# The last two row blocks of a fused attention and feed-forward kernel: product 7 of both blocks ahead of product 4 of both, and the very last rows stored whole

## The chip, the cores and the metric

The kernel runs on one core of one Trainium2 chip. The metric is the device time of one execution in microseconds (us), as a median of several executions. Beside the timed ratio I use a second measure, taken from the profile: the time **from the start of the first matmul of product 7 of row block 0 to the end of the span**. I call it *the end*. Everything that the change touches lies inside it, or at most touches its first moment.

Names in the profile lines: PE is TensorE (matmuls), DVE is VectorE (adds and copies), and SP, ACT and POOL (GpSimd) issue the stores here; a "pair" is the two store issues, of 64 rows each, for one block of 128 rows. A store has landed when the last of its 16 completion signals has arrived.

## The reference, cut to what matters

```python
def reference(q, k, v, omega, w_gate, w_val, w_out):
    attn = performer_attention(q, k, v, omega)        # 8 batches, 8 heads, 576 x 64
    x = attn.transpose(0, 2, 1, 3).reshape(4608, 512)
    g = x @ w_gate                                    # 512 -> 1536
    val = x @ w_val
    return (gelu(g) * val) @ w_out                    # 1536 -> 512, float32
```

Only the last product, for the last rows, matters here.

Of the kernel before, what the change touches and what calls it, by code (L numbers as in the profile page):

```python
# [15 lines left out]
def kernel(  # L16
# [11 lines left out]
    nc = tc.nc  # L28
# [308 lines left out]
    HF, HT = N_DFF // 2, T_TOK // 2  # L337
# [1112 lines left out]
    def end(p):  # L1450

        p.g.sum(0, nc.vector, 0, 3)
        p.g.sum(0, nc.vector, 3, HF)
        p.g.sum(1, nc.vector, 0, HF)
        p.pm(0, 1, 0, HF - 1)
        p.pm(1, 1, 0, HF - 1)
        p.pm(0, 2, 0, HF - 1)
        p.pm(1, 2, 0, HF - 1)
        p.pm(0, 1, HF - 1, HF)
        p.ps_(0, 1, act)  # L1460
        p.pm(1, 1, HF - 1, HF)
        p.ps_(1, 1, act)
        p.pm(0, 2, HF - 1, HF)
        p.pm(1, 2, HF - 1, HF)
        p.g.sum(3, nc.vector, 0, HF)
        p.pm(0, 5, 0, 3)
        p.pm(1, 5, 0, 3)
        p.pm(0, 5, 3, HF)
        p.ps_(0, 5, act)
        p.pm(1, 5, 3, HF)  # L1470
        p.ps_(1, 5, act)
        p.pa(0, 0)
        p.pa(1, 0)
        p.g.sum(2, nc.vector, 0, HF)
        p.pm(0, 6, 0, HF)
        p.ps_(0, 6, act)
        p.pm(1, 6, 0, HF)
        p.ps_(1, 6, act)
        p.pm(0, 3, 0, HF)
        p.pa(0, 1)  # L1480
        p.pst(0, 0, None, (nc.sync, nc.scalar))
        p.pm(1, 3, 0, HF)
        p.pa(1, 1)
        p.pst(1, 0, None, (nc.sync, nc.scalar))
        p.pm(0, 7, 0, HF)
        p.pa(0, 2)
        p.pm(0, 4, 0, HF)
        p.pc(0, dve)
        p.pst(0, 1, None, (nc.sync, nc.scalar))
        p.pm(1, 7, 0, HF)  # L1490
        p.pa(1, 2)
        p.pst(1, 1, 1, (nc.sync, nc.scalar))
        p.pm(1, 4, 0, HF)
        p.pc(1, dve)
        p.pst(1, 1, 0, (nc.sync, nc.scalar))
    E = mybir.EngineType
    with tc.manual_schedule(engines={E.Activation, E.PE, E.DVE, E.SP, E.Pool}):
        g, a = first()
        for t in range(2, N_TOK):
            p = Projection(t - 1, g)  # L1500
            if t + 1 < B:
                n = Attention(t + 2) if t + 2 < B else None
                g, a = step(t, p, a, n), n
            else:
                g = bare(t, p)
        end(Projection(N_TOK - 1, g))
# [30 lines left out]
```

## The kernel before: the parts that the change touches

The kernel takes the 4608 rows in nine groups of 512. The product with `w_out` of the last group is done by a Strassen-like scheme: seven products, numbered 1 to 7, in place of eight, for each of two row blocks `s` (0 and 1) of 128 rows of each half. Product `n` of block `s` is `pm(s, n, ...)`, six matmuls of 128x128 by 128x256. One PSUM tile, `one[s]`, gathers products 1, 6, 7 and 4 one on top of the other, and what it holds is read in between:

```python
def pm(self, s, n, i0, i1):
    ...
    ps = self.two[s][:, 0] if n in (3, 5) else self.two[s][:, 1] if n == 2 else self.one[s]
    for i in range(i0, i1):
        nc.tensor.matmul(ps, x[:, i, s * P:(s + 1) * P], y[:, i], start=n in (1, 2, 5) and i == 0,
                         stop=i == HF - 1, skip_group_check=n not in (1, 2, 5))

def pa(self, s, k):                    # VectorE: o_sb += a PSUM tile
    dst = (self.lo[s][:, :m], self.lo[s][:, m:], self.hi[s][:, m:])[k]
    nc.vector.tensor_add(dst, (self.two[s][:, 1], self.two[s][:, 0], self.one[s])[k], dst)

def pc(self, s, copy):                 # copy one[s], now complete, to the other columns
    copy(self.hi[s][:, :d_model // 2], self.one[s])

def pst(self, s, r, part=None, queues=(nc.sync, nc.sync)):   # store whole rows, or one half of the columns
    ...

def store(c0, o_sb, ns=slice(0, d_model), queues=(nc.sync, nc.sync)):
    for i in range(2):                 # 64 rows each: a pair of issues
        ...
        queues[i].dma_start(out=..., in_=o_sb[i * SP:(i + 1) * SP, :])
```

So `pa(s, 2)` must read `one[s]` after product 7 and before product 4 of the same block. The last lines of the program before the change (cut):

```python
p.pm(0, 7, 0, HF)                               # product 7 of block 0
p.pa(0, 2)                                      # add: reads one[0]
p.pm(0, 4, 0, HF)                               # product 4 of block 0: on top of one[0]
p.pc(0, dve)                                    # copy
p.pst(0, 1, None, (nc.sync, nc.scalar))         # store whole rows
p.pm(1, 7, 0, HF)
p.pa(1, 2)
p.pst(1, 1, 1, (nc.sync, nc.scalar))            # store one half of the columns early
p.pm(1, 4, 0, HF)
p.pc(1, dve)
p.pst(1, 1, 0, (nc.sync, nc.scalar))            # and the other half last
```

The softmax here doesn't subtract the row's maximum and nothing guards it: scores larger than these inputs give would overflow.

## Time and profile before

Times in us after the start of product 7 of block 0, which is at 333.06 of the span (from the trace of before):

| what | block 0 | block 1 |
|---|---|---|
| product 7 starts | 0.00 | 1.99 |
| product 4 starts | 1.33 | 3.32 |
| last copy starts | 2.19 | 4.17 |
| last stores issued (SP and ACT) | 2.64 | 3.29 and 4.62 |
| last landing (SP / ACT) | 4.96 / 5.30 | 6.55 / 6.83 |
| end of the span | | 7.91 |

The median was 343.06 us of three runs, 342.66 to 343.08. The table is read downward: matmuls and VectorE take turns until 4.6, and from there to 7.9 there is only the last store and what follows its landing. The profile lines behind it stand in the prediction.

### The profile page before, as it was taken

How to read it: one execution, taken by the hardware profiler on the slowest of the kernel's cores; microseconds unless marked ns; L12 is line 12 of the kernel's file. 1: busy time of each engine (PE TensorE's matmuls, PEld its weight loads, DVE VectorE, ACT ScalarE, POOL GpSimd, SP SyncE). 2: the span in 40 equal slices, each digit the busy share in tenths (PEclk: the TensorE clock that was granted, in tenths of full speed). 3: DMA queues.
4: the chain of work that ended last, by engine and by line, in shares of the span. 5: the costliest groups of instructions: out<-in, count | busy, mean ns of one | idle time of the engine just before them, and what ended most of it. 6: DMA issues, size and time to landing. Idle time of an engine off the chain costs nothing.

```text
span 341.0 us, 7993 instructions
## 1 busy us (share of the span) xinstructions
PE 327.4 (96%) x3114; PEld 206.0 (60%) x3155; DVE 229.1 (67%) x481; ACT 214.3 (63%) x434; POOL 149.9 (44%) x152
## 2 busy tenths in 40 slices
PE   7889999889999999999999999999999999999994
PEld 3565455566646664566447654665466786686683
DVE  3875388979773768375936683677457777796783
ACT  4894366774778558756875677658765447626640
POOL 8326004033486447744674559477968400000000
PEclk9999999999999999999999999999999999999999
DMA  8999999599889256945498629671413040013004
GB/s 155 275 206 207 206 272 206 137 174 236 178 135 331 49 102 91 326 89 108 60 326 113 116 32 291 164 111 19 94 33 63 8 115 11 1 32 93 2 0 124
DMA packets 67173, 45.08 MB, mean 132 GB/s; under 512 B 47296, under 2 KB 60096, under 8 KB 67136
## 3 DMA queue, kind: packets, MB, share of 16 engines
q0 software_dynamic: 14848, 22.12, 31.4%
q1 hardware_dynamic: 51744, 21.64, 30.4%
q10 hardware_dynamic: 544, 0.82, 0.8%
q8 instruction: 24, 0.39, 0.5%
q14 instruction: 13, 0.11, 0.1%
HBM read 37.78 MB, written 9.44 MB: 138 GB/s over the span
## 4 chain that ended last, share of the span: by engine, by line
PE 83%; DVE 6%; DMA 3%; ACT 3%; issue 2%; POOL 2%; DVEq 0%; POOLq 0%
PE g_ps L433 20%; PE o_ps L559 18%; PE val_one L378 11%; PE val_two L378 9%; PE out_one L533 5%; PE out_two L533 3%; PE v_ps L462 3%; PE g_ps L425 3%; PE kz_ps L285 3%; DMA q_in<-in_q_dram 2%; PE nd L302 2%; PE pk L220 2%; DVE x_sb L314 2%; PE pq L242 2%; DVE val_c L387 1%
## 5 line engine op out<-in xcount | busy, mean ns | idle before, releaser
L433 PE MATMUL g_ps<-xT,w_gate_sb 128*128 128x512 bf16 x352 | 108.2, 379 | 0.5
L440 ACT ACTIVATE g_gelu<-g_ps 128x512 bf16<-128x512 f32 x108 | 63.6, 598 | 54.1 <-PE g_ps L433 25.3
L559 PE MATMUL o_ps<-w_out_sb,gated 128*128 128x512 bf16 x275 | 64.6, 380 | 1.1 <-issue 0.6
L480 POOL TENSOR_TENSOR gated<-g_gelu,val_c 128x512 bf16<-128x512 bf16 x29 | 33.7, 1164 | 52.2 <-DVE iden L313 26.3
L387 DVE TENSOR_TENSOR val_c<-val_one,val_c 128x256 f32<-128x256 f32 x48 | 20.3, 424 | 49.0 <-ACT g_gelu L440 40.0
L378 PEld LDWEIGHTS <-w_val_sb 128*128 128x128 bf16 x384 | 36.5, 98 | 17.3 <-issue 1.4
L559 PEld LDWEIGHTS <-gated 128*128 128x128 bf16 x288 | 26.5, 98 | 33.5 <-issue 3.9
L383 ACT COPY val_c<-val_one 128x256 f32<-128x256 f32 x95 | 35.2, 371 | 11.2 <-PE val_one L378 8.1
L378 PEld LDWEIGHTS <-val_sums 128*128 128x128 bf16 x288 | 27.3, 98 | 24.4 <-DVE x_sb L314 3.7
L249 ACT ACTIVATE q_pT<-pq 128x512 bf16<-128x512 f32 (+1 forms) x68 | 34.6, 598 | 11.7 <-PE pq L242 11.5
L233 DVE TENSOR_REDUCE nmax<-pk 128x8 f32<-128x1024 f32 (+2 forms) x43 | 39.7, 968 | 2.9 <-PE pk L220 1.4
L433 PEld LDWEIGHTS <-w_gate_sb 128*128 128x128 bf16 x376 | 34.9, 98 | 11.2
L228 ACT ACTIVATE k_p<-pk 128x1024 bf16<-128x1024 f32 (+2 forms) x43 | 33.0, 832 | 8.1 <-PE pk L220 6.4
L378 PE MATMUL val_one<-x_sums,w_val_sb 128*128 128x256 bf16 x192 | 36.6, 272 | 0.6 <-DVE val_c L387 0.4
L387 DVE TENSOR_TENSOR val_c<-val_two,val_c 128x256 f32<-128x256 f32 x96 | 36.0, 414 | 0.8 <-PE val_two L378 0.7
L271 POOL TENSOR_TENSOR v_ext<-vf,wk 128x1152 bf16<-128x1152 f32 x12 | 28.2, 2347 | 13.9 <-ACT wk L260 13.9
L484 POOL TENSOR_TENSOR gated<-g_gelu,val_c 128x256 bf16<-128x256 bf16 x34 | 24.1, 711 | 15.0 <-ACT g_gelu L440 15.0
L314 DVE TENSOR_TENSOR x_sb<-nd,iden 128x512 bf16<-128x512 f32 (+2 forms) x41 | 27.8, 677 | 1.4
L564 DVE COPY o_sb<-o_ps 128x512 f32<-128x512 f32 x20 | 13.7, 685 | 19.4 <-PE o_ps L559 14.9
L383 ACT COPY val_c<-val_two 128x256 f32<-128x256 f32 x45 | 16.8, 373 | 11.7 <-PE val_two L378 11.7
L484 DVE TENSOR_TENSOR gated<-g_gelu,val_one 128x256 bf16<-128x256 bf16 x48 | 20.0, 416 | 6.0 <-ACT g_gelu L440 5.7
L378 PE MATMUL val_two<-x_sums,val_sums 128*128 128x256 bf16 x96 | 18.4, 274 | 1.0 <-POOL x_sums L455 0.3
(104 smaller groups left out, 486.3 us busy)
## 6 DMA issues: line engine op xcount, KB each, us to landing
out_dram<-o_sb SPq DMA_DIRECT2D x67, 128.0 KB, 3.3
vf<-in_v_dram POOLq DMA_DIRECT2D x7, 1152.0 KB, 12.4
q_in<-in_q_dram POOLq DMA_DIRECT2D x8, 576.0 KB, 9.4
k_in<-in_k_dram POOLq DMA_DIRECT2D x7, 576.0 KB, 6.2
w_gate_sb<-in_moe_w_gate_dram POOLq DMA_DIRECT2D x3, 512.0 KB, 17.7
w_val_sb<-in_moe_w_val_dram POOLq DMA_DIRECT2D x3, 512.0 KB, 19.4
w_out_sb<-in_moe_w_out_dram POOLq DMA_DIRECT2D x3, 512.0 KB, 13.4
vf<-in_v_dram SPq DMA_DIRECT2D x1, 1152.0 KB, 5.7
```

The costliest lines, as they stand in the source:

```text
L228: last["begun"] = nc.scalar.activation(self.k_p[:, gs, i0:i0 + n, :], pk, func=Exp)
L233: nc.vector.reduce_max(self.nmax[:, gs, i0:i0 + n], pk, axis=AX, negate=True)
L249: last["begun"] = nc.scalar.activation(dst[:, a, i0:i0 + n], self.pq[c][a].rearrange("m (i e p) -> m i e p", e=2, p=SP), func=Exp)
L314: nc.vector.tensor_mul(x_sb[:n].rearrange("p (g h d) -> p g h d", g=2, h=4)[:, gs], ndv[:, :, :, :D], iden[:n, gs].broadcast_to((n, gs.sto ...
L378: nc.tensor.matmul(ps, w[:, c, self.i * P:(self.i + 1) * P], x[:, c], start=first and c == 0, stop=c == 1, skip_group_check=not first)
L383: copy(self.c[:, {1: 0, 6: 1, 5: 2}[n]], self.beta if n == 5 else self.one)
L387: nc.vector.tensor_add(part, (self.gamma, self.beta, self.one)[k], part)
L433: last["begun"] = nc.tensor.matmul(self.gps[jf], w_gate_sb[:, jm, jf * P:(jf + 1) * P], x_tiles[self.t][:, jm], start=(jm == 0), stop=(jm ...
L440: nc.scalar.activation(self.gelus[jf][:, part], src, func=Gelu)
L480: eng.tensor_mul(self.gated[:, i, :], self.gelus[i], self.v[i].row())
L484: eng.tensor_mul(self.gated[:, i + HF, ts], self.gelus[i + HF][:, ts], s.c[:, 2] if half else s.one)
L559: nc.tensor.matmul(self.ps[qq], self.g.gated[:, f, qq * P:(qq + 1) * P], w_out_sb[:, f, :], start=(jf == 0), stop=(jf == N_DFF - 1))
```

## The change

Its intent is to let TensorE work on block 1 while VectorE reads block 0's tile, and to replace the two half-row stores of the last block by one whole-row store.

```diff
         p.pm(0, 7, 0, HF)
         p.pa(0, 2)
+        p.pm(1, 7, 0, HF)
+        p.pa(1, 2)
         p.pm(0, 4, 0, HF)
         p.pc(0, dve)
         p.pst(0, 1, None, (nc.sync, nc.scalar))
-        p.pm(1, 7, 0, HF)
-        p.pa(1, 2)
-        p.pst(1, 1, 1, (nc.sync, nc.scalar))
         p.pm(1, 4, 0, HF)
         p.pc(1, dve)
-        p.pst(1, 1, 0, (nc.sync, nc.scalar))
+        p.pst(1, 1, None, (nc.sync, nc.scalar))
```

## The prediction

> **What bounds the kernel now.** I read the page first. TensorE is busy nearly the whole span, and the chain that ended last is mostly TensorE:
>
> ```profile
> PE 327.4 (96%) x3114; PEld 206.0 (60%) x3155; DVE 229.1 (67%) x481; ACT 214.3 (63%) x434; POOL 149.9 (44%) x152
> ...
> PE 83%; DVE 6%; DMA 3%; ACT 3%; issue 2%; POOL 2%; DVEq 0%; POOLq 0%
> ```
>
> But the change touches only the last two row blocks, so the share over 341.0 us says little. The only slice in which TensorE is not nearly full is the last one (its final digit is 4), and the change lives there. So next the chain of waits, cut to the last 8 us (start, length, what):
>
> ```profile
> 333.22 0.67 PE out_one L533 x6
> 333.89 0.02 issue
> 333.92 0.44 DVE o_sb L544
> 334.35 0.04 issue
> 334.40 1.48 PE out_one L533 x12
> 335.88 0.02 issue
> 335.90 0.43 DVE o_sb L544
> 336.34 0.04 issue
> 336.38 0.83 PE out_one L533 x6
> 337.21 0.02 issue
> 337.23 0.42 DVE o_sb L547
> ```
>
> This is the whole end: product 7 of block 0 (six matmuls), an add on VectorE, then product 4 of block 0 and product 7 of block 1 back to back (twelve), an add, product 4 of block 1, a copy. After that only stores are left. TensorE and VectorE take turns twice, and the reason is in the code: products 7 and 4 of one block accumulate in the same PSUM tile, and the add must read the sum after 7 before 4 may write on top. The timeline of TensorE and of VectorE shows the price of a turn:
>
> ```profile
> 333.92 0.42 DVE L544 TENSOR_TENSOR o_sb<-out_one,o_sb 128x256 f32<-128x256 f32 x1 [0.16 <-PE out_one L533]
> 334.40 0.81 PE L533 MATMUL out_one<-out_sums,gated 128*128 128x256 bf16 x6 [0.52 <-DVE o_sb L544]
> ...
> 336.38 0.81 PE L533 MATMUL out_one<-out_sums,gated 128*128 128x256 bf16 x6 [0.52 <-DVE o_sb L544]
> ...
> 337.23 0.42 DVE L547 COPY o_sb<-out_one 128x256 f32<-128x256 f32 x1 [0.91 <-PE out_one L533]
> ```
>
> In the brackets: TensorE sat idle 0.52 us, twice, and each time the VectorE add released it.
>
> Last, the stores, each one issue on SP and one on ACT, of 64 rows each. The queue's own timeline has five pairs, issued at 333.13, 333.78, 335.70, 336.36 and 337.69 us. Their sizes and median times to landing over the end:
>
> ```profile
> out_dram<-o_sb SPq DMA_DIRECT2D x3, 128.0 KB, 2.3
> out_dram<-o_sb ACTq DMA_DIRECT2D x3, 128.0 KB, 2.7
> out_dram<-o_sb SPq DMA_DIRECT2D x2, 64.0 KB, 2.1
> out_dram<-o_sb ACTq DMA_DIRECT2D x2, 64.0 KB, 2.4
> ```
>
> Taken pair by pair from the same view (SP / ACT): first 2.3 / 2.7, second 2.4 / 3.1, third 2.3 / 2.7 (all whole rows), fourth 2.2 / 2.6, fifth 1.9 / 2.2 (half rows). The fifth pair, issued at 337.69, lands at about 339.6 and 339.9, and the span ends at 341.0.
>
> **What the Trainium skill says.** (1) "Perfetto Trace Analysis", Matmuls: independent matmul groups should rotate through different PSUM banks, so that the evacuation of one runs beside the matmuls of the next. The change does that by order alone: block 1's tile is another tile than block 0's. The trace of before agrees with the other side of it: one tile, and TensorE idle 0.52 us per evacuation. (2) The same page, DMA Instruction — HWDGE: the profiled window of such an issue is descriptor work, not the movement of data, and the completion of a write to HBM can come surprisingly late. The trace agrees: the last issue's window is 0.47 us on SP, its landing 1.9 us. (3) "DMA: Bandwidth & Descriptors", Rules for kernel authors: transfers under 64 KB pay mostly overhead. The trace agrees in kind: the undisturbed 64 KB store (fifth pair) took 1.9 us and the 128 KB one 2.3, so twice the bytes cost 0.4 us more. (4) The same page, Issuing engines are not separate DMA queues: transfers from several engines share the same 16 DMA engines. The trace agrees: in every pair the ACT half lands 0.3 to 0.7 us later than the SP half of the same size, and most so in the second pair, which follows the first after 0.65 us.
>
> **The change part by part.** *Nothing is computed less:* 24 matmuls of these two products, two adds of 0.42 us and two copies of 0.42 us stay. *Moved:* product 7 of block 1 (six matmuls) goes ahead of product 4 of block 0. From the start of the first matmul to the first of the next group when nothing waits: 6 x 0.109 us (0.65 us) by the starts in the trace.
>
> Old order: the last matmul of product 7 of block 0 starts at 333.61; product 4 starts at 334.40. That is 0.79 us where the pitch would be 0.11, so one turn costs 0.68 us (0.31 from that matmul's start to the add's, 0.42 the add, 0.05 until TensorE goes on). The second turn, 335.59 to 336.38, costs 0.68 as well. Together 1.36 us.
>
> New order: product 7 of block 1 starts at 333.72 and its last matmul at 334.26; TensorE would be free for product 4 of block 0 at 334.37. The add of block 0 runs from 333.92 to 334.34 and releases it at 334.40: a wait of 0.03. Product 4 of block 0 thus starts when it does now. The add of block 1 runs from 334.26 + 0.31 = 334.57 to 335.00, released at 335.05; TensorE is free at 334.40 + 0.65 = 335.05: no wait. Product 4 of block 1 starts at 335.05 and not at 336.38. The copies come at 335.25 (as now) and at 335.05 + 0.85 = 335.90; the last ends at 336.33. So **the last store's issue moves from 337.69 to 336.36, 1.33 us earlier**, which is 1.36 less the 0.03.
>
> *Removed:* one of the five pairs of stores, the early half rows of the last block. *Grown:* the last pair, from 64 KB an issue to 128 KB. It is now issued at 336.36, just where the fourth pair stands today, 0.66 us after the third pair at 335.70, which stays whole and stays where it is. There is a twin of that situation in the trace: the second pair, whole rows, issued 0.65 us after a whole first pair on idle queues, took 2.4 and 3.1 us. So the new last pair lands at 336.36 + 2.4 = 338.7 on SP and 336.36 + 3.1 = 339.4 on ACT. Today's last landing is ACT's 339.9. **Of the 1.33 us about 0.85 is given back**, because the last pair is larger and stands close behind another.
>
> *The tail after the landing.* The program ends with SP passing the completion counters of the hardware queues one after the other, 0.06 us each. There are eight, dealt to the stores in turn. Today the first in that list is the last SP store's: it lands at 339.61, SP passes it at 339.63, seven more take until 340.06 (ACT's landing of 339.89 hides among them), and the rest takes 0.91. With two stores fewer the last landing, ACT's, should be on the sixth counter, with only two to pass after it: 339.42 + 0.02 + 0.12 + 0.91 = 340.46. The span would be **340.46 against 340.97: 0.5 us less**.
>
> **The rivals.** (a) *The store hides nothing and the full 1.33 us shows* (about 341.6 us). It needs the last pair to land as fast as today's, 1.9 and 2.2 us. Against it: no whole-row pair took less than 2.3 and 2.7, and this one has the third pair ahead of it. Even with 2.3 and 2.7 the gain would be about 0.9 (342.1). (b) *The larger store eats all of it* (343.0 or a little more). It needs the last ACT store to take 3.5 us or more. For it: the third and the last pair together move 512 KB within some 3 us on shared engines. Against it: the first two pairs did just that and the slower took 3.1. (c) *VectorE becomes the bound of the end:* adds and copies now follow closely. Adds at 333.92 and 334.57, copies at 335.25 and 335.90, each 0.42: no two overlap, gaps of 0.23 us or more, so it would cost nothing. (d) *TensorE still waits:* the second release and the free slot both fall at 335.05, so a release 0.1 us later costs 0.1 us. It is a small term. None of these leaves the 2% band, 6.9 us: the whole stretch that the change touches is 8 us long.
>
> **Range and chances.** Time before 343.06 (three runs, 342.66 to 343.08; the profiled one 342.75). Less 0.5 gives 342.56; the lower runs of before and the chance of a landing faster than the twin pull a little down: 342.5. The rivals put the gain between 0 and 0.9 us, and the runs themselves spread by 0.4: 342.0 to 343.0. Faster or slower by over 2% would need something outside the end to change: 0.005 each.
>
> **What would show it right or wrong.** Right, in the profile of the changed kernel: in the chain of waits the end has one run of some 24 `out_one` matmuls with at most 0.05 us of idle before product 4 of either block; the last `o_sb` copy starts near 335.90; four pairs of stores, the last issued near 336.36 with 2.4 us (SP) and 3.1 us (ACT) to landing; a span near 340.5. The order step is wrong if TensorE shows idle of 0.2 us or more before product 4. The store step is wrong if the last pair lands in under 2.8 us (gain up to 0.9) or over 3.4 us (gain near nothing). The tail step is wrong if more than 1.2 us lie between the last landing and the end. The whole is wrong if anything before 333 us differs by more than 0.2 us between the two traces, since the change gives no cause for it.

## The result, and the profile after

Median 342.74 us of four runs (342.38 to 343.15), against 343.07 of four of before; ratio 0.9991, 95% interval 0.9974 to 1.0008. A ratio here is the mean time of one kernel's fast runs over that of the other's of the same rounds, so it is not quite the ratio of the medians.

The chain of waits after the change, from 333 us on (start, length, what):

```profile
333.71 2.66 PE out_one L533 x24
336.37 0.02 issue
336.39 0.42 DVE o_sb L547
```

The eleven rows of before have become three. The two VectorE adds have left the chain: there is one run of 24 matmuls, then the copy, then the stores. The timeline of the changed kernel shows where the adds went:

```profile
333.55 1.47 PE L533 MATMUL out_one<-w_out_sb,gated 128*128 128x256 bf16 x12
...
334.41 0.42 DVE L544 TENSOR_TENSOR o_sb<-out_one,o_sb 128x256 f32<-128x256 f32 x1 [0.16 <-PE out_one L533]
334.88 1.47 PE L533 MATMUL out_one<-out_sums,gated 128*128 128x256 bf16 x12
335.06 0.42 DVE L544 TENSOR_TENSOR o_sb<-out_one,o_sb 128x256 f32<-128x256 f32 x1 [0.23 <-PE out_one L533]
...
336.39 0.42 DVE L547 COPY o_sb<-out_one 128x256 f32<-128x256 f32 x1 [0.23 <-PE out_one L533]
```

Matmuls of both product 7s stand in one row (x12), those of both product 4s in the next, and the second carries no idle time in brackets. The adds, at 334.41 and 335.06, lie beside matmuls.

The last pair of stores, from the same kernel's DMA view cut to its issue (KB, then us to landing):

```profile
out_dram<-o_sb SPq DMA_DIRECT2D x1, 128.0 KB, 2.3
out_dram<-o_sb ACTq DMA_DIRECT2D x1, 128.0 KB, 3.0
```

Before, the last pair was 64 KB each and took 1.9 and 2.2. Two windows of each kernel, split at the start of the end, hold the balance. Columns: window, its length, then busy time and count of PE, PEld, DVE, ACT and POOL, the clock, the DMA share and GB/s. The windows of before:

```profile
30.00:333.06 303.06, 298.41 (x2755) 187.07 (x2793) 208.36 (x437) 191.78 (x393) 134.02 (x129) 1.00 0.59 124
...
333.06:341.00 7.94, 3.10 (x26) 2.24 (x23) 2.16 (x6) 0.00 (x0) 0.00 (x0) 0.90 0.46 133
```

And of the changed kernel:

```profile
30.50:333.55 303.05, 298.40 (x2755) 186.95 (x2793) 208.48 (x437) 191.69 (x393) 133.67 (x129) 1.00 0.59 124
...
333.55:341.00 7.45, 2.81 (x26) 2.24 (x23) 2.17 (x6) 0.00 (x0) 0.00 (x0) 1.00 0.47 142
```

(The windows were cut at 341.00; exactly, the end is 7.91 us before and 7.31 after.) The 303 us in the middle are the same to 0.01 us, and the same 2755 matmuls lie in them. But the changed kernel arrives at this point 0.49 us later, because its first 30 us took 0.5 us longer in that execution. So the two spans differ by only 0.1 us (340.97 and 340.86), although the end itself is **0.60 us shorter**. Whether those 0.5 us belong to the change is one of the questions for the experiments. The granted clock of 0.90 in the last window of before has no part in it: the record falls to 0.5 only at 339.33 us, after the last matmul has started (336.92), and in both kernels matmuls that do not wait start 0.109 us apart.

### The profile page after: what moved, and what is told of

It reads as the page before. It is cut to its first block, busy times and chain, and to the rows that moved or that the text cites. A ratio compares the mean times of both kernels' runs of the same rounds, so it can differ in the third digit from the quotient of the medians.

```text
span 340.9 us, 7989 instructions
## 1 busy us (share of the span) xinstructions
PE 328.0 (96%) x3114; PEld 206.8 (61%) x3155; DVE 229.2 (67%) x481; ACT 214.2 (63%) x434; POOL 149.8 (44%) x152
## 4 chain that ended last, share of the span: by engine, by line
PE 83%; DVE 8%; ACT 2%; issue 2%; DMA 2%; POOL 1%; SPq 0%; DVEq 0%; POOLq 0%
PE g_ps L433 20%; PE o_ps L559 18%; PE val_one L378 11%; PE val_two L378 9%; PE out_one L533 5%; PE out_two L533 3%; PE v_ps L462 3%; PE g_ps L425 3%; PE kz_ps L285 3%; PE pk L220 2%; DVE nmax L233 2%; PE nd L302 2%; DVE x_sb L314 2%; PE pq L242 2%; DVE val_c L387 1%
```

## The experiments

My theory: the order alone is worth 1.33 us at the last issue; the whole-row store gives part of it back, partly by its size and partly because it stands close behind another pair; a small part of the end depends on which completion counter the last store has. The rivals: the store's size costs nothing; the reorder is eaten by crowded queues; the late start of the end comes from the change. Here is what all profiled executions gave, in us after the start of product 7 of block 0. "Start" is where that lies in the span.

| kernel | start | last issue (SP / ACT) | its landing (SP / ACT) | end |
|---|---|---|---|---|
| before | 333.06 | 4.62 / 4.63 | 6.55 / 6.83 | 7.91 |
| changed | 333.55 | 3.29 / 3.30 | 5.62 / 6.28 | 7.31 |
| changed, again | 333.46 | 3.30 / 3.30 | 5.61 / 6.26 | 7.29 |
| changed, third | 333.80 | 3.30 / 3.30 | 5.62 / 6.28 | 7.31 |
| order alone | 333.43 | 3.29 / 3.44 | 5.76 / 5.95 | 7.12 |
| store alone | 333.50 | 4.62 / 4.63 | 6.94 / 7.26 | 8.30 |
| third pair on GpSimd | 333.39 | 3.29 / 3.30 | 5.97 / 6.85 | 8.01 |
| counters turned | 333.31 | 3.29 / 3.30 | 5.66 / 6.27 | 7.57 |
| order, halves, counters | 333.08 | 3.29 / 3.45 | 5.49 / 5.81 | 6.86 |
| the same, again | 333.22 | 3.29 / 3.45 | 5.50 / 5.84 | 6.89 |
| early half on GpSimd | 333.56 | 3.30 / 3.30 | 5.96 / 6.13 | 7.15 |
| queue by block | 333.28 | SP twice: 3.29, 3.82 | 5.62, 6.43 | 7.43 |

### Order alone

```diff
 # against the changed kernel
         p.pm(1, 7, 0, HF)
         p.pa(1, 2)
+        p.pst(1, 1, 1, (nc.sync, nc.scalar))
         p.pm(0, 4, 0, HF)
         ...
         p.pc(1, dve)
-        p.pst(1, 1, None, (nc.sync, nc.scalar))
+        p.pst(1, 1, 0, (nc.sync, nc.scalar))
```

> Products reordered as in the changed kernel, but the last rows still stored in two halves: the early half right after its add, the late half after the copy. Everything is counted from the start of the first matmul of product 7 of block 0 to the end of the span (before: 7.91 us, changed kernel: 7.31 us). My theory (order worth 1.33 us, the larger last store gives part back): the last issue is 3.30 us after that start, half rows land in 2.2 (SP) and 2.6 us (ACT) as the fourth pair of before did, and the end comes at 6.9 us, 1.0 us shorter than before and 0.4 shorter than the changed kernel. Rival (three pairs at 0.65 us spacing clog the queues): the last pair takes 2.6 and 3.0 us or more and the end comes at 7.3 us or later, no better than the changed kernel.

Measured: 342.58 us median of five (before: 343.56 of nine), ratio 0.9969, interval 0.9955 to 0.9982. The last issue on SP is at 3.29, as expected, and the end comes at 7.12: 0.79 us shorter than before and 0.19 shorter than the changed kernel. I had expected 6.9. The missing 0.2 is in the last pair, which took 2.47 us on SP where I had put 2.2:

```profile
out_dram<-o_sb SPq DMA_DIRECT2D x1, 64.0 KB, 2.5
out_dram<-o_sb ACTq DMA_DIRECT2D x1, 64.0 KB, 2.5
```

On ACT it also went out 0.15 us late (3.44), because ACT was still on its issue of the pair before, 0.70 us long. So the rival, crowded queues, is right about a part: half the bytes did not bring the 1.9 and 2.2 us of before. But it does not eat the gain. (A part of the 2.47 us is peculiar to this trace, see "Order, halves and counters".)

### Store alone

```diff
 # against the kernel before
-        p.pst(1, 1, 1, (nc.sync, nc.scalar))
         p.pm(1, 4, 0, HF)
         p.pc(1, dve)
-        p.pst(1, 1, 0, (nc.sync, nc.scalar))
+        p.pst(1, 1, None, (nc.sync, nc.scalar))
```

> Old order of products, but the last rows stored whole. My theory: the last issue stays 4.63 us after the start of product 7 of block 0; the whole rows, 2 us behind the pair before, land in 2.3 (SP) and 2.7 us (ACT); 1.05 us of tail; the end comes at 8.35 us, 0.4 us longer than before. Rival (the size of the last store costs nothing, because fixed cost is all): 1.9 and 2.2 us to landing, the end at 7.9 us as before.

Measured: 343.62 us median, ratio 1.0006, interval 0.9993 to 1.0018, and the end at 8.30 us where I had expected 8.35. The chain of waits has both turns again; its last rows:

```profile
336.34 0.43 DVE o_sb L544
336.78 0.04 issue
336.82 0.83 PE out_one L533 x6
337.65 0.02 issue
337.67 0.42 DVE o_sb L547
```

And the last pair, two us behind the pair ahead of it:

```profile
out_dram<-o_sb SPq DMA_DIRECT2D x1, 128.0 KB, 2.3
out_dram<-o_sb ACTq DMA_DIRECT2D x1, 128.0 KB, 2.6
```

This run separates size from closeness, with the exact figures of the trace. On ACT the last store took 2.20 us with half rows apart from others (before, 1.33 us behind the pair ahead), 2.64 with whole rows apart (here, 1.98 us behind) and 2.98 with whole rows 0.65 us behind another pair (changed kernel). **Taken in this order, the size costs 0.44 us and the closeness 0.34.** On SP the size costs 0.39 (1.93 to 2.32) and the closeness nothing (2.33). The two do not simply add: half rows close behind another pair took 2.20 us on SP and 2.36 on ACT (order, halves and counters, below, with ACT's issue 0.15 us later), so there the closeness costs 0.27 on SP and the step to whole rows 0.62 on ACT. The rival that the size is free has fallen, and the two parts of the change act in opposite directions: the new order shortens the end, the larger last store lengthens it.

### Third pair on GpSimd

```diff
 # against the changed kernel
-        p.pst(0, 1, None, (nc.sync, nc.scalar))
+        p.pst(0, 1, None, (nc.gpsimd, nc.gpsimd))
```

> The changed kernel with the pair of stores ahead of the last issued from GpSimd, so that the last pair is alone on the two hardware queues. If the 2.98 us of the last ACT store come from standing close behind another pair on the same queues, it falls to 2.7 us (SP to 2.3), and the end comes at 7.15 to 7.2 us (four counters are left to pass in place of two), unless the GpSimd stores land later than that. Rival (it comes from the shared 16 DMA engines and the memory): still 2.9 to 3.0 us, the end at 7.4 us or later.

Measured: 343.33 us median, ratio 0.9998, interval 0.9981 to 1.0015, the end at 8.01 us. **Both expectations missed.** The last pair did not get faster or stay, it got slower:

```profile
out_dram<-o_sb POOLq DMA_DIRECT2D x2, 128.0 KB, 2.7
out_dram<-o_sb SPq DMA_DIRECT2D x1, 128.0 KB, 2.7
out_dram<-o_sb ACTq DMA_DIRECT2D x1, 128.0 KB, 3.6
```

In the trace's packet records the first packet of the last ACT store moves 2.36 us after its issue, against 1.75 in the store-alone run and 1.85 in the changed kernel. The two GpSimd stores were issued one after the other, at 2.92 and 3.51 us, so the second went out after the last pair (3.29) and not ahead of it. Stores from GpSimd are therefore not a way round the two hardware queues here. Why they delay that first packet the runs do not show.

### Counters turned

```diff
 # against the changed kernel, in the call for an earlier group of rows (made twice)
-        p.pst(1, 1)
+        p.pst(1, 1, 0)
+        p.pst(1, 1, 1)
```

The program gives the stores its eight hardware completion counters in turn, and at the end SP passes all of them in a fixed order. Two more pairs earlier on turn this by four, so that the last ACT store has the second counter in place of the sixth.

> The changed kernel with two earlier stores (tens of us before the end) split in halves, which turns the completion counters by four: the last ACT store is on the second counter of the list, with six to pass after it in place of two. My theory of the tail: 1.28 us from the last ACT landing to the end in place of 1.03, all else in the end the same, so 7.55 us from product 7 of block 0. Rival (the tail is a fixed cost after the last landing): 1.03 us and 7.3 us.

Measured: one run, 342.66 us (its state is unknown, so only its trace is read), end 7.57 us. The last landing is where it was (6.27 against 6.28), and the end came 1.30 us after it and not 1.03. The expectation was 1.28; the rival, a fixed cost after the last landing, has fallen. After a landing SP passes one counter each 0.06 us, so here it was worth 0.26 us to have the last store sixth in that order and not second.

### The changed kernel again

No edit.

> The changed kernel once more, timed in more rounds, because 0.9991 with an interval of 0.9974 to 1.0008 does not separate it from before. My theory: the end again comes 7.3 us after the start of product 7 of block 0 (0.6 us shorter than before), and the ratio is 0.9983 give or take 0.001; where product 7 starts (333.06 in before, 333.55 in the changed kernel) is jitter of the first 30 us and may be anything from 333.0 to 333.6. Rival (the change itself moves the start of product 7 by 0.5 us): again 333.5 to 333.6, and a ratio of 0.9995 or more.

Measured: 342.54 us median of five against 342.96 of nine, ratio 0.9983, interval 0.9970 to 0.9995. The end is 7.29 us. In eleven of the twelve profiles of the table the start of the end lies between 333.08 and 333.80; the twelfth, that of before, happened to be the earliest at 333.06. The order-and-halves kernel, which has the new order too, started at 333.08, and the store-alone kernel, which has the old order, at 333.50. From the first `o_sb` copy on VectorE (96.2 to 97.0 us) to the start of product 7 it is 236.83 to 236.86 us in every one of them. So the 0.49 us is jitter of the early part and no effect of the change. It is not all of the first 30 us, as I had expected: ScalarE's first `o_sb` copy starts at 53.74 us in the first and in the third profile of the changed kernel, and product 7 starts 0.25 us later in the third.

### Order, halves and counters

```diff
 # against the order-alone kernel, in the last call for an earlier group of rows
-        p.pst(1, 0)
+        for part in (1, 0) if p.t == N_TOK - 2 else (None,):
+            p.pst(1, 0, part)
 # and likewise p.pst(0, 1) and p.pst(1, 1)
```

> The order-alone kernel with three earlier pairs of stores (tens of us before the end) split in halves, which turns the counters by six, so that only two (ACT) and one (SP) are left to pass after the last landings. Its last pair landed 5.76 (SP) and 5.95 us (ACT) after the start of product 7. My theory of the tail: the end comes 1.05 us after the ACT landing, at 7.0 us in place of 7.12; ratio 0.997. Rival (the tail is what it is): 7.1 us.

Measured: 342.46 us median, ratio 0.9983, interval 0.9970 to 0.9997, the end 6.86 us. The end comes 1.05 us after the ACT landing, as expected. But the landings were also 0.14 (ACT) and 0.27 (SP) earlier than in the order-alone run, though the stores of the end are the same:

```profile
out_dram<-o_sb SPq DMA_DIRECT2D x1, 64.0 KB, 2.2
out_dram<-o_sb ACTq DMA_DIRECT2D x1, 64.0 KB, 2.4
```

That part I did not expect. A second profile of this kernel gave 5.50 and 5.84 again. The trace of order alone shows where the difference sits. In its last six stores, one of the 16 completion signals comes 0.11 to 0.40 us behind the other 15; on SP's last store the 15th comes at 5.49 us, where the whole store had landed here, and the 16th at 5.76. In both profiles of this kernel the 16th is at most 0.05 us behind. And the DMA view of the end of order alone has a row that both profiles of this kernel lack:

```profile
q14 instruction: 1, 0.01, 0.4%
```

It is one packet of 8 KB, which starts at 3.02 us and takes 0.52 us, while 103 packets of the stores move beside it. In the other traces that have it, it takes 0.31 to 0.35 us beside 16 to 28 packets. That it held one piece of each store back fits the times, but no run moves it alone, so it is not shown.

Against the changed kernel, which has the same order and nearly the same tail (1.03 us), the last landing is 0.44 to 0.46 us earlier in the two profiles: that is what storing the whole rows last costs at this place.

### Early half on GpSimd

```diff
 # against the order-alone kernel
-        p.pst(1, 1, 1, (nc.sync, nc.scalar))
+        p.pst(1, 1, 1, (nc.gpsimd, nc.gpsimd))
```

> The order-alone kernel with the early half rows of the last block issued from GpSimd. If the two hardware queues were what held its last pair back (2.47 and 2.66 us from the issue at 3.29), the pair now lands in 2.2 and 2.6 us and the end comes at 6.95 us. If stores issued from GpSimd hold the hardware queues back, as the run with the third pair on GpSimd suggests (3.55 us for the last ACT store), the last ACT store takes 3.0 us or more and the end comes at 7.3 us or later.

Measured: 342.31 us median of four, ratio 0.9978, interval 0.9964 to 0.9991, the end 7.15 us. The last pair took 2.7 us on SP and 2.8 on ACT, between the two expectations, so this run is **inconclusive** on why GpSimd disturbs. It shows that taking two of the six last stores off the hardware queues did not free them: the pair was slower than in the order-alone run.

### Queue by block

```diff
 # against the changed kernel
-        p.pst(0, 1, None, (nc.sync, nc.scalar))
+        p.pst(0, 1, None, (nc.scalar, nc.scalar))
...
-        p.pst(1, 1, None, (nc.sync, nc.scalar))
+        p.pst(1, 1, None, (nc.sync, nc.sync))
```

> The changed kernel with both stores of the pair ahead of the last on ACT and both of the last on SP. If the two queues work through their descriptors independently of each other, the SP stores (issued at 3.29 and about 3.76) land in 2.3 us each, the last at 6.1, and the end comes at 7.15 us. If all four share what makes descriptors and moves data, the order of arrival is all and the last lands at 6.3 us or later, the end at 7.3 us or later.

Measured: one run, 342.48 us (its state is unknown, so only its trace is read), the end 7.43 us. The last store, the second on SP, landed at 6.43, 2.61 us after its issue at 3.82, and the second store on ACT took 2.83 us. Independent queues with 2.3 us each would have landed it at 6.1: that forecast has fallen. Of the 0.3 us that it missed, 0.06 is the issue (3.82 and not 3.76). Whether the rest comes from the store ahead on the same queue or from those on the other, the run does not tell.

It shows one thing more. The first ACT store, issued 0.65 us ahead of any SP store, landed in 2.26 us, and its first packet moved 1.14 us after its issue. In the changed kernel, where an SP store is issued at the same moment, the same ACT store took 2.66 us and its first packet 1.76. So ACT's later landing in the other runs goes with the SP store issued at the same moment, and not with a slower queue.

### The two side by side

Two more runs on one chip: the changed kernel and the order with halves and counters.

> The changed kernel on the same chip as the next run, to compare the two directly. The end again 7.3 us after the start of product 7 of block 0; ratio to before 0.998 to 0.999.

> The order with the last rows in halves and the counters turned, once more, beside the changed kernel. By the traces (6.86 against 7.29 us from the start of product 7 to the end) it should be about 0.4 us, 0.12%, faster than the changed kernel and about 1.0 us, 0.3%, faster than before. Rival (what the trace shows in the end of one execution does not carry to the median, or the split of earlier stores costs it back): no difference from the changed kernel, as in the batch before (0.9983 for both).

Measured: the changed kernel 342.89 us median, ratio 0.9992 (0.9979 to 1.0005), end 7.31; the other 342.58 us, ratio 0.9983 (0.9969 to 0.9997), end 6.89. Over the two batches that had both, ten runs each, the means are 342.63 and 342.42, 0.21 us apart, where the ends are 0.43 apart, and the runs of one kernel scatter with a standard deviation of 0.33 to 0.34 us. With ten runs each the standard error of that difference is 0.15 us, so the traces say clearly that this version ends sooner than both kernels, and the timed runs agree in direction without deciding it against the changed kernel. Against before its interval excludes 1 in both batches. Over order alone, timed in another batch at 0.9969, it shows no timed advantage.

## Why the prediction was right

The prediction was 342.5 us, 0.5 us less than before. The changed kernel was timed three times beside before: 0.33, 0.42 and 0.40 us less by the medians, with ratios 0.9991, 0.9983 and 0.9992; only the second of their intervals excludes 1. The 0.60 us of the traces would be a ratio of 0.9983, which lies in all three. The timed number alone says little: the stated range, 342.0 to 343.0, reaches nearly from the full gain to none, and four runs of the changed kernel spread over 0.77 us. What carries the mechanism is the traces, with one profile of before and three of the changed kernel (ends of 7.29 to 7.31). By steps:

- **The order, 1.33 us at the last issue: right.** The last issue moved from 4.62 to 3.29 us. The 0.03 us of waiting that should stay ahead of product 4 of block 0 is there (its start is 1.33 us after product 7's, as forecast), and product 4 of block 1 starts 0.66 us later (1.99), with no idle time shown.
- **The store, 0.85 given back: right in mechanism, slightly too large.** I had taken it whole from a twin, the second pair of before, at 3.06 us. It measured 2.98, so 0.78 us were given back on ACT. The prediction named two causes without parting them; the store-alone run parts them into 0.44 for size and 0.34 for closeness, taken in that order.
- **The tail, 1.05 us after the last landing: right.** It measured 1.03, and 1.30 when the counters were turned, as the working by counters asks. Before it was 1.08 from the ACT landing (7.91 less 6.83), since the counter of the SP store, first in the list, was what SP waited for there.
- **The sum.** -1.33 + 0.78 - 0.05 = -0.60 us, the measured change of the end. I had 0.50 on the same terms (-1.33 + 0.86 - 0.03).
- **The rivals.** The full 1.33 us did not show (a), nor was all of it eaten (b). VectorE did not become the bound (c): no two of its last four instructions touch, the gaps are 0.23 to 0.25 us. TensorE does not wait (d).
- **What I had wrong is a check, not a term of the sum:** "anything before 333 us differs by more than 0.2 us" was to show the whole wrong. It differed by 0.49 us. The runs showed that the arrival at that point scatters over 0.7 us with the same work ahead of it. I had set that limit without a second trace of before to tell me how far two executions differ. The forecast span missed for the same reason: 340.86 us and not 340.46, which is 0.49 of late start less 0.09 of larger gain.

## What to carry to other kernels

Where a PSUM tile is read in the middle of its accumulation, put another block's matmuls between the two, and work out from the starts in the trace whether they are long enough to cover the read: here six matmuls of 0.11 us covered all but 0.03 us of an add of 0.42 us with its hand-overs. At the very end of a program, what counts is the landing of the last store and not its issue: a larger last store, close behind another one, gave back 0.78 of 1.33 us. So the two parts of this change are better taken apart: the new order alone ended 0.79 us sooner than before, and with the whole-row store 0.60. When an effect is smaller than the scatter of the runs, align two traces on a common instruction and compare only what follows it.

## What the Trainium skill lacked or had wrong

- "DMA: Bandwidth & Descriptors", Latency and other measured facts, gives about 600 ns to the first byte for the hardware path. In the trace of before the first packet of the first 64-row store to HBM of the end moved 1.13 us after the start of its issue on SP (333.128 to 334.256 us), and 1.76 us after on ACT, issued at the same time. The page does not say from which moment it counts: from the end of the issue's window on SP (0.47 us) it is 0.66 us, near its figure, so no more is shown than that the figure is not to be counted from the start of an issue.
- The same page, Issuing engines are not separate DMA queues, says that transfers interleave, but has no figure for a store close behind another: 2.64 us apart and 2.98 us when issued 0.65 us after another pair (ACT queue, 128 KB). Nor has it one for two stores issued at the same moment on SP and ACT: ACT's first packet moved after 1.76 us in the changed kernel, and after 1.14 in the run in which ACT's store went first.
- No page that I read says that stores issued from GpSimd can delay those on the SP and ACT queues: the last ACT store took 3.55 us with two GpSimd stores issued around it, and 2.98 with two hardware-queue stores 0.65 us ahead of it in their place.
- No page that I read says that the order in which the completion counters are passed at the end is worth time: the tail after the last landing was 1.03 us with two counters left to pass and 1.30 us with six.
